# A gated scan and two feed-forward layers on one core: gates and weight sums moved to GpSimd, two plain groups in the second unit in place of three

## The chip, the core and the metric

The kernel runs on one core of a Trainium2 chip. The metric is the device time of one execution in microseconds; before the change it is 1969.47, the median of three runs (1969.35 to 1969.48). The engines are written as in the profile: PE (TensorE's matmuls), PEld (its weight loads), DVE (VectorE), ACT (ScalarE), POOL (GpSimd) and SP, whose queue issues nearly all of the DMAs.

## The reference

```python
def _attn_ref(x, f_logit, lower_bound):          # 2 x 6080 x 256
    sig = 1.0 / (1.0 + np.exp(-f_logit))
    f = lower_bound[None, None, :] + (1.0 - lower_bound[None, None, :]) * sig
    i = 1.0 - f
    for t in range(S):
        h = f[:, t] * h + i[:, t] * x[:, t]
        y[:, t] = h
def _moe_ref(x, w_in, w_out):                    # 12160 x 256, 2048 wide
    h = np.maximum(x @ w_in, 0.0)
    return h * h @ w_out
def _moe2_ref(x, w_in, w_out):
    h = x @ w_in
    g = np.where(h > 0.0, h, alpha * (np.exp(np.minimum(h, 0.0)) - 1.0))
    return g @ w_out
```

The scan feeds the first layer (m = 0), and that one feeds the second (m = 1). All in float32.

## The kernel before, in words

**Tiles.** The 12160 tokens are cut into 12 units: the first has 512 + 384 tokens, all others 512 + 512. Each layer goes unit by unit and, inside a unit, through eight groups g of its 2048 inner columns. The second layer follows the first five units behind.

**Precision.** Each float32 operand of a matmul is split into a high part (rounded to float32r, by ACT or as a DVE cast) and a low part (DVE subtraction, lines 467, 542, 901 and 401). Every product is then three matmuls (`three`, line 854).

**Two forms of a group's first matrix product.** A group multiplies a 2 x 2 block of weights with a 2 x 2 block of inputs (two halves of the tokens, two halves of the 256 inputs). In the *plain* form that is 4 products for each half of the tokens, 8 in all, or 24 matmuls (`add_plain`). In the *other* form it is 7 products, or 21 matmuls (`open_slot`, `add_product`, in the order of `PATTERN`), for which sums and differences of the inputs (lines 601 and 542) and of the weights (`weight_sums`, four 128x128 operations, lines 375 to 378) have to be there first, and the results of which are added up by DVE from PSUM (line 1081). The second matrix product takes 24 matmuls for a group in both forms (line 1138). `plain` (line 243) uses the plain form for the whole of the first unit of the first layer and for the groups below `PLAIN_G` of its second unit.

**Weights.** `add_weights` loads and rebuilds a group's weights. For the first layer it keeps them in DRAM (`keep` in `wd`, `keep_whole` in `rd`); `add_sums` (line 502) later loads `rd`, makes the sums, splits them and writes them to `wd` too. `add_stream` then loads the split weights of each slot from `wd` to `ws`. For the second layer `add_weights` makes the sums itself.

**Scan.** Each unit has four chunks of 256 tokens (`add_scan`, line 693). A chunk is loaded, goes through a tanh on ACT (line 738), two transposes on DVE (line 758, `xT` and `fT`), two gates on 128x256 (line 767, `fT` in place), `feed` (line 775) and two scans (line 788). The first unit has its own path, whose gates are on ACT and DVE.

**Order.** Every step is given to a planner (`Order`) with an engine, an estimated duration and a due time. It runs a simulated clock and writes each engine's instructions in the order in which they came out. On the chip every engine, SP's queue among them, runs its own in that fixed order, and waits at each instruction until its inputs are there. POOL has no step in the plan before the change.

Of the kernel before, what the change touches and what calls it, by code (L numbers as in the profile page):

```python
# [13 lines left out]
ALU = mybir.AluOpType  # L14
PSUM = bass.MemoryType.PSUM

P = 128
# [1 line left out]
CN = 256  # L19
SIZES = ((512, 384), (512, 512))  # L20
LEAD = 2
PLAIN_G = 3
TLATE = 75.0
SLATE = 4.0
GAP = 56
# [41 lines left out]
class Order:  # L67
# [47 lines left out]
    def run(self):  # L115
        steps = self.steps
        after = self.after
        for (tag, k), n in self.first.items():
            steps[n][4].update(self.users.get((tag, k - BUFS[tag]), ()))
            if k and self.first[tag, k - 1] != n:  # L120
                after.add((self.first[tag, k - 1], n))
        for p, n in after:
            steps[n][4].add(p)
        users = [[] for _ in steps]
        wait = [len(s[4]) for s in steps]
        for n, s in enumerate(steps):
            for p in s[4]:
                users[p].append(n)
        free = {"PE": 0.0, "ACT": 0.0, "DVE": 0.0, "SP": 0.0}
        ends = [None] * len(steps)  # L130
        began = [None] * len(steps)
        moved = 0.0
        ready = {e: {} for e in free}

        def offer(n):
            s = steps[n]
            for e in [s[0]] + ([s[5][0]] if s[5] else []):
                t = 0.0
                for p in s[4]:
                    pe, pt = ends[p]  # L140
                    lat = self.LOAD + self.MORE * (pt > 25.0) if pe == "SP" else self.CROSS if pe != e else 0.0 if e == "PE" else self.SAME
                    t = max(t, began[p] if (p, n) in after else pt + lat)
                ready[e][n] = t

        for n, w in enumerate(wait):
            if not w:
                offer(n)
        order = []
        while any(ready.values()):
            best = None  # L150
            for e, r in ready.items():
                if not r:
                    continue
                t0 = max(free[e], min(r.values()))
                n = min((n for n, t in r.items() if t <= t0 + self.HOLD), key=lambda n: steps[n][2])
                if t0 < self.RAMP:
                    late = t0 > self.CALM
                    v = min((n for n, t in r.items() if t <= t0 + self.WAIT[late]), key=lambda n: steps[n][2])
                    if steps[v][2] < steps[n][2] - self.FAR[late]:
                        n = v  # L160
                t0 = max(t0, r[n])
                if best is None or t0 < best[0]:
                    best = (t0, e, n)
            t0, e, n = best
            s = steps[n]
            us = s[1] if e == s[0] else s[5][1]
            free[e] = t0 + us
            began[n] = t0
            ends[n] = (e, t0 + us)
            if s[6]:  # L170
                moved = max(moved, t0 + us / 2) + s[6] / (self.FIRST if moved < 6.0 else self.RATE if moved < 25.0 else self.LATER)
                ends[n] = ("SP", max(moved, t0 + us))
                if e == "SP":
                    free[e] = max(free[e], moved - self.AHEAD)
            for r in ready.values():
                r.pop(n, None)
            order.append((n, e))
            for u in users[n]:
                wait[u] -= 1
                if not wait[u]:  # L180
                    offer(u)
        assert len(order) == len(steps)
        for n, e in order:
            steps[n][3](e)
# [3 lines left out]
def kernel(  # L188
# [11 lines left out]
    nc = tc.nc  # L200
# [3 lines left out]
    KD = D // P  # L204
# [38 lines left out]
    def plain(m, u, g=0):  # L243
        return m == 0 and (u == 0 or u < PLAIN and g < PLAIN_G)

# [4 lines left out]
    rd = [dram.tile([P, 4, P], F32, name=f"rd{g}") for g in range(KG)]  # L250
    xd = [dram.tile([P, KD, sum(ns)], F32, name=f"xd{u}") for u, ns in enumerate(units)]

    def new(tag, shape, dtype=F32):
        return pools[tag].tile(shape, dtype, tag=tag, name=tag)
# [82 lines left out]
    order = Order()  # L337

    def act(n, psum=False):
        return (0.05 if psum else 0.09) + n / 1172  # L340

    def dve(n, fast=False, psum=False):
        return (0.12 if psum else 0.067) + n / (1920 if fast else 960)

    def chain(due, steps):

        left = sum(st[1] + order.SLACK for st in steps)
        for e, us, what, *rest in steps:
            order.add(e, us, due - left, what, *rest)
            left -= us + order.SLACK  # L350
# [3 lines left out]
    def key_of(tag):  # L354
        count[tag] = count.get(tag, -1) + 1
        return tag, count[tag]
# [15 lines left out]
            queue.dma_start(st.rearrange("p k e w -> p k (e w)"), v)  # L372

    def weight_sums(q, a):
        nc.vector.tensor_tensor(q[:, 0], a[:, 0], a[:, 2], op=ALU.add)
        nc.vector.tensor_tensor(q[:, 2], a[:, 1], a[:, 0], op=ALU.subtract)
        nc.vector.tensor_tensor(q[:, 1], q[:, 0], a[:, 1], op=ALU.subtract)
        nc.vector.tensor_tensor(q[:, 3], a[:, 3], q[:, 1], op=ALU.subtract)

    def plain_weights(key):  # L380

# [7 lines left out]
    def add_kept_parts(t, x, key, m, c, at, due):  # L389

        w = key_of("wp")

        def high_part(e):
            t["w" + x] = new("wp", [P, 4, P], F32R)
            if e == "ACT":
                nc.scalar.activation(t["w" + x], t[x], AF.Copy)
            else:
                nc.vector.tensor_copy(t["w" + x], t[x])

        def low_part(e):  # L400
            nc.vector.tensor_tensor(t[x].bitcast(F32R), t[x], t["w" + x].bitcast(F32), op=ALU.subtract)

        def keep(e):
            nc.sync.dma_start(wd[m][c][:, 0, at : at + 4].bitcast(F32), t["w" + x].bitcast(F32))
            nc.sync.dma_start(wd[m][c][:, 1, at : at + 4].bitcast(F32), t[x])

        chain(due, [
            ["DVE", dve(CE, True), high_part, [key], [w], ("ACT", act(CE))],
            ["DVE", dve(CE), low_part, [w], [key]],
            ["SP", 1.0, keep, [w, key], [("wd", m, c, at)], None, 512],  # L410
        ])

    def add_weights(i, m, kind, c, due, wk=None):
# [58 lines left out]
        def keep_whole(e):  # L472
            nc.sync.dma_start(rd[c], t["a"])

        st, a = ("st", i), key_of("a")
        steps = [
            ["SP", 0.475, load, (), [st], None, 512],
            ["ACT", act(CE), scaled, [st], [a]],
            ["ACT", act(CE), low_bits, (), [st]],
            ["DVE", dve(CE), magnitude, [st], [a]],  # L480
            ["DVE", dve(CE), sign, [st], [a]],
        ]
# [2 lines left out]
            del steps[0]  # L485
        if m == 1 and kind == 0:
            q = key_of("a")
            chain(due - 6.0, [*steps, ["DVE", 4 * dve(P), sums, [a], [q]]])
            add_kept_parts(t, "a", a, m, c, 0, due - 2.0)
            add_kept_parts(t, "q", q, m, c, 4, due)  # L490
            return
# [5 lines left out]
        ])  # L497
        if kind == 0:
            order.add("SP", 0.5, due + 16.0, keep, [w], [("wd", m, c, 0)], None, 512)
            order.add("SP", 0.5, due + 10.0, keep_whole, [a], [("rd", c)], None, 256)  # L500

    def add_sums(c, due):

        t = {}

        def load(e):
            t["a"] = new("a", [P, 4, P])
            nc.sync.dma_start(t["a"], rd[c])

        def sums(e):  # L510
            t["q"] = new("a", [P, 4, P])
            weight_sums(t["q"], t["a"])

        a, q = key_of("a"), key_of("a")
        chain(due - 4.0, [
            ["SP", 0.5, load, [("rd", c)], [a], None, 256],
            ["DVE", 4 * dve(P), sums, [a], [q]],
        ])
        add_kept_parts(t, "q", q, 0, c, 4, due)

# [172 lines left out]
    def add_scan(i, u, h, q, due, after=None, from_=None):  # L693
        at, n = chunks(u, h)[q]
# [66 lines left out]
        def gate(c):  # L761
            def go(e):
                f, a, b = t["fT"], ga[:, c : c + 1], gb[:, c : c + 1]
                if e == "ACT":
                    nc.scalar.activation(f[:, c], f[:, c], AF.Identity, scale=a, bias=b)
                else:
                    nc.vector.tensor_scalar(f[:, c], f[:, c], a, b, op0=ALU.mult, op1=ALU.add)  # L767
            return go

        def bound(e):  # L770
# [30 lines left out]
        fs, xs, fT, xT = (("fs", i), ("xs", i), ("fT", i), ("xT", i))  # L801
# [3 lines left out]
        if u == 0:  # L805
# [34 lines left out]
            ["ACT", act(N), tanh, (), [fs]],  # L840
            ["DVE", dve(N), turn("xs", "xT"), [xs], [xT], None, 0, after],
            ["DVE", dve(N), turn("fs", "fT"), [fs], [fT], None, 0, after],
            *(["DVE", dve(n), gate(c), [("bound",)], [fT]] for c in range(KD)),
            ["DVE", dve(N), feed, [fT], [xT]],
            *(["DVE", 0.1 + n / 490, scan(c), [fT, xT, ("carry",), ("scan",), *opened], [F, (*F, c), ("scan",)]] for c in range(KD)),
            *([["DVE", 0.1, carry_on, [F], [("carry",)]]] if h * q else []),
# [418 lines left out]
    def begin_unit(s):  # L1265
# [12 lines left out]
        elif u in mixed and m == 0:  # L1278
            if s == (m, u, None, PLAIN_G):
                add_later_parts(u, mixed[u], s)  # L1280
# [49 lines left out]
```

## Time and profile before

| | |
|---|---|
| median of three runs | 1969.47 us (1969.35 to 1969.48) |
| span of the profiled execution (first to last instruction) | 1968.4 us |
| median less span: what lies around the span | 1.07 us |
| busy: PE, ACT, DVE, POOL | 1955.5, 1627.1, 1498.6, 0.7 us |
| PE waits for other engines and DMAs, whole run | 8.4 us in 5 waits |

The page gives the profiled execution by its span alone; its own time is taken as that span and the 1.07 us around it, which is the median of the runs. PE's busy time counts a matmul from its modelled start to its modelled end, and matmuls overlap in the pipeline, so the number of matmuls times the step between them says more of PE than the busy share.

### The profile page before, as it was taken

Reading aid. Unit: us, or ns where it says so; the run is one execution under the profiler, and the core shown is the slowest. Engines: PE = TensorE matmul, PEld = TensorE weight load, DVE = VectorE, ACT = ScalarE, POOL = GpSimd, SP = SyncE. Lnnn points to the kernel's source line nnn. Section 1 sums busy time; section 2 is a strip of 40 time slices with the busy share of each in tenths; the row PEclk is TensorE's granted clock in tenths of the full one; section 3 lists DMA queues with packets and bytes.
Section 4 is the critical chain, followed back from the end, with each engine's and each line's share of the span. In section 5 each row is a group of like instructions: output and inputs, shape, how many; then the busy total and the mean of one; then the engine's idle time right before and its main releaser. Section 6 shows DMA issues by size and latency. Waiting matters only on the chain.

```text
span 1968.4 us, 23749 instructions
## 1 busy us (share of the span) xinstructions
PE 1955.5 (99%) x8713; PEld 1631.7 (83%) x8713; DVE 1498.6 (76%) x1933; ACT 1627.1 (83%) x2181; POOL 0.7 (0%) x6
## 2 busy tenths in 40 slices
PE   8999999999999999999999999999999999999999
PEld 7888888888888888888888888888888888888888
DVE  7998899867876876777777687687775668778686
ACT  8989999888888878878878887887887878878786
POOL 0000000000000000000000000000000000000000
PEclk9999999999999999999999999999999999999999
DMA  8876675532533434353254343334423324243332
GB/s 259 241 225 210 206 226 176 170 128 94 145 128 115 114 119 137 102 149 132 81 146 128 113 131 113 126 104 126 137 94 102 126 99 137 94 134 99 113 116 74
DMA packets 228868, 269.21 MB, mean 137 GB/s; under 512 B 151952, under 2 KB 154512, under 8 KB 228752
## 3 DMA queue, kind: packets, MB, share of 16 engines
q1 hardware_dynamic: 226752, 267.24, 43.2%
q8 instruction: 68, 1.11, 0.2%
q10 hardware_dynamic: 2000, 0.46, 0.1%
q14 instruction: 48, 0.39, 0.1%
HBM read 223.87 MB, written 43.78 MB: 136 GB/s over the span
## 4 chain that ended last, share of the span: by engine, by line
PE 99%; DVE 1%; DMA 0%; ACT 0%; issue 0%; SPq 0%; DVEq 0%
PE a L1138 53%; PE c L856 46%; DMA st<-in_moe_w_in_dram 0%; DVE F L788 0%; DVE a L432 0%; DVE a L435 0%; DVE xT L749 0%; DVE o L1177 0%; DVE xa L542 0%; SPq L701 0%; DVE F L467 0%; DVE fT L767 0%; DVE ws L467 0%; ACT a L426 0%; ACT st L429 0%
## 5 line engine op out<-in xcount | busy, mean ns | idle before, releaser
L1138 PE MATMUL a<-g,wo 128*128 128x512 f32 (+2 forms) x4608 | 1155.7, 387 | 0.0
L1138 PEld LDWEIGHTS a<-g,wo 128*128 128x128 f32 x4608 | 863.8, 188 | 171.2
L1074 ACT ACTIVATE r<-c 128x512 f32<-128x512 f32 (+1 forms) x724 | 423.4, 585 | 251.0 <-PE c L856 245.0
L901 DVE TENSOR_TENSOR g<-r,g 128x1024 fp32r<-128x1024 f32 (+2 forms) x382 | 461.6, 1208 | 142.1 <-ACT g L896 134.4
L1081 DVE TENSOR_TENSOR r<-c,r 128x512 f32<-128x512 f32 (+1 forms) x543 | 371.6, 684 | 191.7 <-PE c L856 187.7
L896 ACT ACTIVATE g<-r 128x1024 fp32r<-128x1024 f32 (+2 forms) x382 | 402.9, 1055 | 67.1 <-PE a L1138 50.4
L856 PE MATMUL c<-xa,ws 128*128 128x512 f32 (+2 forms) x1713 | 445.3, 387 | 1.1 <-DVE ws L467 0.6
L856 PEld LDWEIGHTS c<-xa,ws 128*128 128x128 f32 x1713 | 320.5, 188 | 65.9 <-DVE ws L467 1.0
L856 PE MATMUL c<-xb,ws 128*128 128x512 f32 (+2 forms) x1146 | 316.3, 386 | 0.0
L891 DVE SCALAR_TENSOR_TENSOR r<-e,r 128x1024 f32<-128x1024 f32 (+1 forms) x190 | 230.8, 1215 | 105.3 <-ACT e L888 105.3
L856 PE MATMUL c<-xc,ws 128*128 128x512 f32 (+1 forms) x1098 | 307.1, 388 | 0.0
L856 PEld LDWEIGHTS c<-xb,ws 128*128 128x128 f32 x1146 | 214.6, 188 | 42.0
L856 PEld LDWEIGHTS c<-xc,ws 128*128 128x128 f32 x1098 | 206.1, 188 | 41.9
L881 ACT ACTIVATE r<-r 128x1024 f32<-128x1024 f32 (+1 forms) x192 | 201.0, 1048 | 0.3
L888 ACT ACTIVATE e<-e 128x1024 f32<-128x1024 f32 (+1 forms) x190 | 198.5, 1045 | 0.7
L885 ACT ACTIVATE e<-r 128x1024 f32<-128x1024 f32 (+1 forms) x190 | 197.2, 1042 | 0.4
L875 ACT ACTIVATE r<-r 128x1024 f32<-128x1024 f32 x85 | 89.4, 1051 | 0.0
L601 DVE TENSOR_TENSOR F<-F 128x512 f32<-128x512 f32 (+1 forms) x92 | 62.9, 683 | 1.0
L788 DVE TENSOR_TENSOR_SCAN F<-fT,F,xT 128x256 f32<-128x256 f32 (+1 forms) x72 | 52.2, 736 | 0.7
L878 ACT ACTIVATE r<-r 128x512 f32<-128x512 f32 x85 | 52.7, 620 | 0.0
L542 DVE TENSOR_TENSOR xa<-F,xa 128x512 fp32r<-128x512 f32 (+3 forms) x49 | 44.9, 923 | 0.4
L767 DVE TENSOR_SCALAR fT<-fT,ga,gb 128x256 f32<-128x256 f32 x90 | 33.7, 404 | 0.9
(72 smaller groups left out, 608.1 us busy)
## 6 DMA issues: line engine op xcount, KB each, us to landing
ws<-wd SPq DMA_DIRECT2D x181, 896.0 KB, 4.9
xd<-o SPq DMA_DIRECT2D x46, 256.0 KB, 2.8
fs<-in_f_logit_dram SPq DMA_DIRECT2D x176, 64.0 KB, 2.3
xs<-in_x_dram SPq DMA_DIRECT2D x176, 64.0 KB, 2.6
F<-xd SPq DMA_DIRECT2D x22, 512.0 KB, 4.7
out_dram<-o SPq DMA_DIRECT2D x88, 128.0 KB, 5.3
st<-in_moe_w_in_dram SPq DMA_DIRECT2D x16, 512.0 KB, 5.5
st<-in_moe_w_out_dram SPq DMA_DIRECT2D x16, 512.0 KB, 4.8
```

What stands on the lines that cost most here:

```text
L601: nc.vector.tensor_tensor(f[:, to], f[:, i], f[:, k], op=ALU.subtract)
L856: nc.tensor.matmul(out, lhsT=ws[:, p, w], rhs=xs[:, r, v], start=start and q == 0, stop=stop and q == 2, skip_group_check=check,)
L875: nc.scalar.activation(r_t[0], r_t[0], AF.Relu)
L881: nc.scalar.activation(r_t[0], r_t[0], AF.Square)
L885: nc.scalar.activation(t["e"], r_t[0], AF.Relu, scale=-1.0)
L888: nc.scalar.activation(t["e"], t["e"], AF.Exp, scale=-1.0)
L891: nc.vector.scalar_tensor_tensor(r_t[0], t["e"], 1.0, r_t[0], op0=ALU.subtract, op1=ALU.max)
L896: nc.scalar.activation(g_t[s, which][:, 0], r_t[0], AF.Copy)
L901: nc.vector.tensor_tensor(g_t[s, which][:, 1], r_t[0], g_t[s, which][:, 0].bitcast(F32), op=ALU.subtract)
L1074: nc.scalar.activation(r[0][:, i], t[A], f)
L1081: nc.vector.tensor_tensor(r[:, i], t[tag], r[:, i], op=ALU.add)
L1138: nc.tensor.matmul(a, lhsT=y, rhs=v, start=begin and jj == 0 and p == 0, stop=end and jj == len(mine) - 1 and p == 2, skip_group_check=True,)
```

## The change

It does four things. The gates of all units but the first, and the sums of the weights of both layers, are GpSimd instructions (`engine.tensor_scalar` and `nc.gpsimd.tensor_tensor`), and the planner gets a POOL engine with an estimate of its own. `PLAIN_G` is 2, so that group 2 of the second unit has the form with seven products. The write of the whole weights to `rd` is due 7 us earlier.

```diff
-PLAIN_G = 3
+PLAIN_G = 2
...
-        free = {"PE": 0.0, "ACT": 0.0, "DVE": 0.0, "SP": 0.0}
+        free = {"PE": 0.0, "ACT": 0.0, "DVE": 0.0, "POOL": 0.0, "SP": 0.0}
...
+    def pool(n):
+        return 0.15 + n / 900
...
     def weight_sums(q, a):
-        nc.vector.tensor_tensor(q[:, 0], a[:, 0], a[:, 2], op=ALU.add)
-        nc.vector.tensor_tensor(q[:, 2], a[:, 1], a[:, 0], op=ALU.subtract)
-        nc.vector.tensor_tensor(q[:, 1], q[:, 0], a[:, 1], op=ALU.subtract)
-        nc.vector.tensor_tensor(q[:, 3], a[:, 3], q[:, 1], op=ALU.subtract)
+        nc.gpsimd.tensor_tensor(q[:, 0], a[:, 0], a[:, 2], op=ALU.add)
+        nc.gpsimd.tensor_tensor(q[:, 2], a[:, 1], a[:, 0], op=ALU.subtract)
+        nc.gpsimd.tensor_tensor(q[:, 1], q[:, 0], a[:, 1], op=ALU.subtract)
+        nc.gpsimd.tensor_tensor(q[:, 3], a[:, 3], q[:, 1], op=ALU.subtract)
...
-            chain(due - 6.0, [*steps, ["DVE", 4 * dve(P), sums, [a], [q]]])
+            chain(due - 6.0, [*steps, ["POOL", 4 * pool(2 * P), sums, [a], [q]]])
...
-            order.add("SP", 0.5, due + 10.0, keep_whole, [a], [("rd", c)], None, 256)
+            order.add("SP", 0.5, due + 3.0, keep_whole, [a], [("rd", c)], None, 256)
...
-            ["DVE", 4 * dve(P), sums, [a], [q]],
+            ["POOL", 4 * pool(2 * P), sums, [a], [q]],
...
-                    nc.vector.tensor_scalar(f[:, c], f[:, c], a, b, op0=ALU.mult, op1=ALU.add)
+                    engine = nc.gpsimd if e == "POOL" else nc.vector
+                    engine.tensor_scalar(f[:, c], f[:, c], a, b, op0=ALU.mult, op1=ALU.add)
...
-            *(["DVE", dve(n), gate(c), [("bound",)], [fT]] for c in range(KD)),
+            *(["POOL", pool(n), gate(c), [("bound",)], [fT]] for c in range(KD)),
```

In the changed kernel's rows line numbers are 3 higher from line 345 and 4 higher from line 768 on: 542 is 545, 758 is 761, 775 is 779, 788 is 792, 901 is 905, 1081 is 1085, 1138 is 1142. In all, 88 gates and 64 sums stand on POOL, and DVE has 88 and 64 fewer; matmuls are 8710, from 8713.

**A chunk of the scan in a late unit, DVE.** Before:

```order
L758 STREAM_TRANSPOSE xT<-xs 128x8x2x32
L758 STREAM_TRANSPOSE fT<-fs 128x8x2x32
L767 TENSOR_SCALAR fT<-fT,ga,gb 128x256 x2
L775 SCALAR_TENSOR_TENSOR xT<-fT,xT 128x512
L788 SCALAR_TENSOR_TENSOR F_8677<-fT,F_8677,xT 128x256
L901 TENSOR_TENSOR g<-r,g 128x1024
L1081 TENSOR_TENSOR r<-c_8903,r 128x512
```

The same place of the changed kernel:

```order
L761 STREAM_TRANSPOSE xT<-xs 128x8x2x32
L761 STREAM_TRANSPOSE fT<-fs 128x8x2x32
L779 SCALAR_TENSOR_TENSOR xT<-fT,xT 128x512
L792 SCALAR_TENSOR_TENSOR F_8680<-fT,F_8680,xT 128x256
L905 TENSOR_TENSOR g<-r,g 128x1024
L1085 TENSOR_TENSOR r<-c_8904,r 128x512
```

The two gates are gone from DVE's queue, and in this chunk nothing has come in their place: `feed` stands right behind the transpose, and waits for POOL.

**Where the second unit takes up the other form, DVE.** `F_829` holds the scan's result of the second unit, `xa`, `xb` and `xc` its split inputs; the rows of 128x512 for `xb` and `xc` are the raw second half, the row of 128x1024 is the differences of products 4 and 3. The changed kernel:

```order
L545 TENSOR_TENSOR xb<-F_829,xb 128x512
L545 TENSOR_TENSOR xc<-F_829,xc 128x512
L470 TENSOR_TENSOR wo_71<-a,wo_71 128x2x256
L604 TENSOR_TENSOR F_829<-F_829 128x512
L905 TENSOR_TENSOR g<-r,g 128x2x384
...
L404 TENSOR_TENSOR a<-a,wp 128x512 x2
L905 TENSOR_TENSOR g<-r,g 128x1024
L761 STREAM_TRANSPOSE fT<-fs 128x8x2x32
L545 TENSOR_TENSOR xb<-F_829,xb 128x1024
```

Between the second row and the last stand 14 instructions; before the change 33 stood there, 12 of them sums and 2 gates.

**The same place on POOL**, from its first gates on:

```order
L771 TENSOR_SCALAR fT<-fT,ga,gb 128x256 x3
L378 TENSOR_TENSOR a<-a 128x128
L379 TENSOR_TENSOR a<-a 128x128
L380 TENSOR_TENSOR a<-a 128x128
L381 TENSOR_TENSOR a<-a 128x128
L771 TENSOR_SCALAR fT<-fT,ga,gb 128x256 x3
L378 TENSOR_TENSOR a<-a 128x128
```

Gates and sums share one queue: a gate of the second unit's second chunk stands behind the first group's four sums, which wait for their own load.

## Rows read from the trace of the kernel before

**Rows 1.** The page: span, busy time of engines, granted clock by slice.

```profile
span 1968.4 us, 23749 instructions
...
PE 1955.5 (99%) x8713; PEld 1631.7 (83%) x8713; DVE 1498.6 (76%) x1933; ACT 1627.1 (83%) x2181; POOL 0.7 (0%) x6
...
PEclk9999999999999999999999999999999999999999
```

**Rows 2.** Waits of PE: line, waited for, us in total, times, longest.

```profile
PE c L712 <- DMA fs<-in_f_logit_dram: 6.6, 2, 3.9
PE a L712 <- DMA fs<-in_f_logit_dram: 0.7, 1, 0.7
PE c L856 <- DVE ws L467: 0.6, 1, 0.6
PE c L856 <- DVE xa L542: 0.5, 1, 0.5
```

**Rows 3.** The chain that ended last: start us, us, what.

```profile
21.60 6.78 PE c L856 x34
...
118.62 2.04 PE a L1138 x9
...
128.82 2.04 PE a L1138 x9
...
1954.07 9.13 PE a L1138 x45
```

**Rows 4.** Windows, four of 20 us from 60 to 140 us: busy us of each engine.

```profile
sum 80.00, PE 80.00 PEld 68.91 DVE 77.96 ACT 68.36 POOL 0.00; mean PE 20.00 PEld 17.23 DVE 19.49 ACT 17.09 POOL 0.00
```

**Rows 5.** Groups of DVE instructions, 60 to 140 us: count, busy us, mean ns.

```profile
L767 DVE TENSOR_SCALAR fT<-fT,ga,gb 128x256 f32<-128x256 f32 x16 | 6.2, 400 | 0.0
...
L378 DVE TENSOR_TENSOR a<-a 128x128 f32<-128x128 f32 x8 | 2.3, 292 | 0.3
...
L375 DVE TENSOR_TENSOR a<-a 128x128 f32<-128x128 f32 x8 | 2.3, 281 | 0.9 <-DMA a<-rd 0.9
```

**Rows 6.** Groups of the whole run: gates on ACT, what POOL ran.

```profile
L765 ACT ACTIVATE fT<-fT,gb,ga 128x256 f32<-128x256 f32 (+1 forms) x6 | 3.4, 565 | 0.2
...
masks.py:199 POOL TENSOR_SCALAR_AFFINE_SELECT one<-one 128x128 f32<-128x128 f32 x1 | 0.3, 294 | 0.1
masks.py:197 POOL MEMSET one<- 128x128 f32 x1 | 0.2, 205 | 0.3 <-POOLq L1316 0.3
...
L1316 POOL MEMSET const-uint8-127<- 128x1 uint8 x1 | 0.1, 102 | 0.0
```

**Rows 7.** Timeline of a late chunk: start us, us, engine, line, what.

```profile
1026.03 0.67 DVE L758 STREAM_TRANSPOSE fT<-fs 128x512 f32<-128x512 f32 x1
...
1027.50 0.69 DVE L775 SCALAR_TENSOR_TENSOR xT<-fT,xT 128x512 f32<-128x512 f32 x1
...
1029.60 1.23 DVE L901 TENSOR_TENSOR g<-r,g 128x1024 fp32r<-128x1024 f32 x1 [0.61 <-ACT g L896]
1030.74 0.68 DVE L1081 TENSOR_TENSOR r<-c,r 128x512 f32<-128x512 f32 x1
...
1032.38 0.84 PE L856 MATMUL c<-xc,ws 128*128 128x512 f32 x3
```

**Rows 8.** Timeline where the second unit changes form.

```profile
94.45 2.88 PE L856 MATMUL c<-xa,ws 128*128 128x512 f32 x12
...
96.16 0.69 DVE L542 TENSOR_TENSOR xc<-F,xc 128x512 fp32r<-128x512 f32 x1
...
99.27 0.86 PE L856 MATMUL c<-xb,ws 128*128 128x512 f32 x3
...
114.45 1.22 DVE L542 TENSOR_TENSOR xb<-F,xb 128x1024 fp32r<-128x1024 f32 x1
...
117.78 0.84 PE L856 MATMUL c<-xb,ws 128*128 128x512 f32 x3
```

**Rows 9.** Timeline of SP's queue: the first DMA at which its order changes.

```profile
19.29 0.39 SPq L366 DMA_DIRECT2D st<-in_moe_w_out_dram  x1
```

## The prediction

> **What bounds the kernel now.** Read the page first. PE is busy for 1955.5 of 1968.4 us, its granted clock is at the upper level, 2.4 GHz, in every slice, DVE has 24% to spare over the run, and POOL ran 0.7 us [rows 1]. So the question is only what PE still waits for, and the view of waits answers it: 8.4 us in five waits, two for the first tokens' loads and two for the first unit's weights and inputs [rows 2]. The chain of waits agrees: from 21.60 us to PE's last work (1954.07 + 9.13 = 1963.2) it is PE alone, one stretch of matmuls after the other [rows 3]. The time is therefore a count of matmuls times a step. The chain gives the step: a group of the form with seven products, with its second product, is 21 + 24 = 45 matmuls and comes back after 128.82 - 118.62 = 10.20 us [rows 3], so one matmul of 512 columns takes 10.20 / 45 = 0.2267 us. (The 0.39 us that the groups of instructions give for one matmul is a length in a pipeline, not a step.)
>
> Nothing that is taken off DVE shortens that chain by itself. What it can do is keep PE fed where DVE was nearly full: from 60 to 140 us DVE was busy for 77.96 of 80 us [rows 4], while PE never waited. There the change works.
>
> **The change part by part.**
>
> *Two plain groups, not three.* Group 2 of the second unit takes 21 matmuls in place of 24 for its first product, and 24 for its second as before. PE loses 3 matmuls: 3 x 0.2267 = 0.68 us, straight off the chain. DVE gets three more additions from PSUM (0.68 us each, as in [rows 7]), ACT four evacuations more of one kind and four fewer of another; both have room.
>
> *Gates and sums off DVE.* In 60 to 140 us DVE ran 16 gates (6.2 us) and 8 sets of four sums (four groups of 2.3 us, 9.2 us) [rows 5]; 15.4 us at most go from 78, since busy times of neighbours overlap a little. On the path of PE this is worth nothing: it waited for none of it. Over the run DVE loses 88 gates of 0.40 us and 64 sums of 0.29 us, some 54 us.
>
> *The same on POOL.* The trace has no gate on POOL, so I bound one. Below: a MEMSET of 128 columns took 0.205 us and one of a single column 0.102, which is 0.81 ns a column, so 256 columns take 0.31 us; it only writes. Nearest, since it reads and writes: the AFFINE_SELECT of 128 columns, 0.294 us, is 1.51 ns a column, so a gate takes 0.49 us. Above: twice that rate, 0.88 us. ACT's gate takes 0.565 us, inside these bounds [rows 6]. A sum has 128 columns and two inputs: 0.205 below, 0.49 with the read counted twice, 0.88 above. I take 0.49 us for both, as the nearest row has it. 152 of them are 74 us of 1968 on an engine that did nothing.
>
> *The wait that this adds.* `feed` now waits on DVE for two gates on POOL, and everything behind it on DVE waits too. In the late chunk, DVE's transpose ends at 1026.70 and `feed` starts at 1027.50: the gates cost 0.80 us [rows 7]. On POOL they cost 2 x 0.49 and two handovers; the trace has none with POOL, but DVE took 0.04 us after ACT in this very stretch (an estimate of 0.2 us would be generous). That is 1.06 us, with 0.2 us each 1.38: `feed` comes 0.26 to 0.58 us later. Behind it stand the scan and line 901, before which DVE sat idle for 0.61 us [rows 7], which covers it. If a gate took 0.88 us, `feed` would come 1.04 us later with the short handover, 901 0.43 us later, and then the addition of line 1081; it ended at 1031.42, and the matmul that takes that bank again (product 1) starts at 1032.38, 0.96 us after [rows 7]. So PE still would not wait. Cost 0; the cover is the 0.61 and the 0.96 us, and it is gone when a gate costs more than (0.80 + 0.61 + 0.96 - 0.08) / 2 = 1.14 us.
>
> *The second unit changes form one group earlier.* One plain group is gone ahead of it, so two things are wanted earlier. The raw second half (`xb`, `xc`) was wanted at 99.27 us and is wanted where group 2's plain product started, at 94.45, 4.82 us earlier. `xc` was ready at 96.85, and PE took it 0.70 us after `xb`, at 99.97; now it is wanted at 95.15 [rows 8]. That needs 1.70 us off DVE's work; 8 of the 16 gates and 3 of the 8 sets stood ahead, 8 x 0.40 + 12 x 0.287 = 6.6 us [rows 5]. Margin 4.9 us. The differences (128x1024) were wanted at 117.78 and are wanted 48 x 0.2267 = 10.9 us earlier, at 106.9 [rows 8]. The changed order has 14 instructions between `xc` and them; 11 of about 0.69 us, three of 1.23 us and their own 1.22 us are 12.5 us [rows 7, 8], counted from 96.85 - 6.6 = 90.25 that is 102.8. Margin 4.1 us. Cost 0, between 0 and some 3 us if the freed time is partly lost.
>
> *The earlier write to `rd`.* On SP it moves ahead of a load of weights, first at 19.29 us [rows 9]. An issue takes about 0.4 us, so the load comes that much later; from 21.60 us on PE waited for no weight [rows 3]. Three such places lie in the first unit: 0 to 1.2 us, I take 0.
>
> **Sum.** 1968.4 + 1.07 us around the span is the median of the runs, 1969.47. Less 0.68 it is **1968.8 us**, 0.03% less. About 0.2%, 3.9 us, is what a measurement of this kernel can tell from no change, so my forecast is "no change that can be told". Its own range, with that cost at 1.2 us and the runs' spread of 0.1 to both sides, is 1968.7 to 1970.1.
>
> **The rivals.**
>
> *A. The handover comes late.* POOL's queue is in order, and a gate of the second chunk stands behind the first four sums, which wait for their load. If this, or the load, costs more than the margin of 4.1 us, PE pays the rest one for one. For: DVE did idle 0.9 us for that very load [rows 5]. Against: twice that and four sums (2.0 us) are still inside. I price it in the middle of what stays under 3.9 us, +1.9: 1970.7.
>
> *B. POOL and DVE block each other.* DVE frees time, but each POOL instruction makes DVE stand still for as long. Up to `xc` that is 8 gates and 12 sums, 20 x 0.49 = 9.8 us back for 6.6 us saved; `xc` then comes at 96.85 - 6.6 + 9.8 = 100.05 and is wanted at 95.15: PE waits 4.9 us, 1973.7, slower. At ACT's price for a gate (0.565) it is 6.4 us, 1975.2. It decides from half of it on: with 0.245 us of standstill for each instruction the 4.9 us of margin are just used up. Later the kernel has idle DVE time at each chunk, and loses nothing. For: DVE is near its limit there [rows 4]. Against: while `feed` waits for a gate, DVE stands idle and cannot be blocked. The trace has no two of them side by side.
>
> The Trainium skill has such a rule ("SBUF — State Buffer", section "Who interferes with whom"): a DVE instruction with two inputs in SBUF contends with a GpSimd instruction that reads SBUF, and the second to issue waits. By that rule DVE's subtractions and `feed` would meet gates and sums, its transposes and its additions from PSUM would not, and the time would be B's instead of mine. No run here shows it.
>
> *C. A gate on POOL is slow.* Above 1.14 us a gate, each of the 36 chunks of the units behind the third costs PE what is over. At 1.4 us that is 2 x 0.26 x 36 = 18.7 us: 1987.5, slower. For: no row prices it. Against: it would be nearly five times the AFFINE_SELECT for twice the columns.
>
> *D. Faster by over 0.2%.* That would need 3.9 us off PE. PE's waits are 8.4 us, all in the first unit [rows 2], which the change leaves as it is. Only matmuls count, and three go. It would be 1965.5 or less.
>
> **How the numbers follow.** Forecast 0.62; A 0.18; B 0.10; C 0.07; D 0.03. Faster 0.03, same 0.62 + 0.18 = 0.80, slower 0.10 + 0.07 = 0.17. The likeliest time is 1968.8. The range goes from 1968.3, a little under the forecast, through A up to B's 1973.7, say 1974; outside it are C, half of B and D, 0.15.
>
> **What would show it.** Right: PE 8710 matmuls, its waits the same four kinds and about 8.4 us, the form of 45 matmuls in the second unit from about 104 us on, 74 us or less on POOL, some 1445 us on DVE. In the chunk, DVE idle before `feed`, waiting for POOL, and no wait of PE for `r` behind it. A shows as one wait of PE near 84, 94 or 107 us for `xa`, `xb`, `xc` or `ws`. B shows as gates, sums or subtractions much longer between 60 and 110 us than alone, C as gates over 1.1 us and PE waiting for line 1081's result in every unit. The prediction is wrong if PE's waits grow by over 4 us, or if the step of a matmul changes.

## The result and the profile after

| | before | after |
|---|---|---|
| median | 1969.48 us (1969.35 to 1970.0) | 1980.14 us (1979.02 to 1980.69, 5 runs) |
| ratio | | 1.0051, 95% interval 1.0041 to 1.0062 |
| span of the profiled execution | 1968.4 us | 1977.4 us (of 1979.35) |

The change makes the kernel 0.5% slower, 10.7 us. The prediction was 1968.8, with 1968.3 to 1974.0 as its range: wrong, and by far more than the 3.9 us that can be told from no change.

First the page of the changed kernel, which answers to [rows 1]: span, busy time, and two of its costliest groups (busy us, mean ns, idle before and what ended it).

```profile
span 1977.4 us, 23864 instructions
...
PE 1959.2 (99%) x8710; PEld 1631.9 (83%) x8710; DVE 1462.4 (74%) x1782; ACT 1625.3 (82%) x2185; POOL 103.1 (5%) x158
...
L771 POOL TENSOR_SCALAR fT<-fT,ga,gb 128x256 f32<-128x256 f32 x88 | 62.5, 719 | 1128.1 <-DVE fT L761 1128.1
...
L779 DVE SCALAR_TENSOR_TENSOR xT<-fT,xT 128x512 f32<-128x512 f32 x44 | 30.6, 694 | 36.1 <-POOL fT L771 35.9
```

The three matmuls are gone, DVE is relieved of 36 us, and `feed` waits for POOL 36 us in all. That is not where the time went. PE's waits after the first unit tell it (line, waited for, us, times, longest); before, none but the first unit's [rows 2]:

```profile
PE a L1142 <- ACT wo L464: 3.8, 1, 3.8
PE c L860 <- DVE r L1085: 0.7, 2, 0.4
PE a L1142 <- DVE g L905: 0.6, 1, 0.6
```

PE is held up from 87 us on. Windows of 20 us from 60 to 140 us show the place (busy us of each engine, then granted clock):

```profile
80.00:100.00 20.00, 15.59 (x63) 12.05 (x62) 15.99 (x25) 13.49 (x22) 9.20 (x13) 0.91 0.70 230
100.00:120.00 20.00, 20.00 (x95) 17.18 (x94) 13.50 (x17) 15.31 (x24) 8.53 (x15) 1.00 0.68 211
...
sum 80.00, PE 74.78 PEld 62.28 DVE 59.25 ACT 62.45 POOL 32.35; mean PE 18.70 PEld 15.57 DVE 14.81 ACT 15.61 POOL 8.09
```

DVE, busy for 77.96 of these 80 us before [rows 4], is now busy for 59.25: 18.7 us less, more than the 15.4 that went to POOL. It is not short of time, it stands and waits. The timeline of the changed kernel shows for what (start us, us, engine, line; in brackets the idle time before and what ended it):

```profile
72.20 5.52 SPq L737 DMA_DIRECT2D xs<-in_x_dram  x8
...
78.45 1.02 SPq L511 DMA_DIRECT2D a<-rd  x2
...
83.19 0.46 POOL L378 TENSOR_TENSOR a<-a 128x128 f32<-128x128 f32 x1 [5.30 <-issue]
...
84.57 0.46 POOL L381 TENSOR_TENSOR a<-a 128x128 f32<-128x128 f32 x1
85.06 0.63 ACT L399 ACTIVATE wp<-a 128x512 fp32r<-128x512 f32 x1 [4.96 <-POOL a L381]
...
85.60 0.83 ACT L900 ACTIVATE g<-r 128x768 fp32r<-128x768 f32 x1
...
86.46 1.05 DVE L905 TENSOR_TENSOR g<-r,g 128x768 fp32r<-128x768 f32 x1 [3.90 <-ACT g L900]
...
87.57 2.17 PE L1142 MATMUL a<-g,wo 128*128 128x384 f32 x11 [0.64 <-DVE g L905]
87.81 2.84 POOL L771 TENSOR_SCALAR fT<-fT,ga,gb 128x256 f32<-128x256 f32 x2
...
95.59 0.63 ACT L464 ACTIVATE wo<-a 128x512 fp32r<-128x512 f32 x1 [0.68 <-DVE a L438]
...
96.27 4.70 PE L1142 MATMUL a<-g,wo 128*128 128x512 f32 x12 [3.77 <-ACT wo L464]
...
97.73 0.55 POOL L378 TENSOR_TENSOR a<-a 128x128 f32<-128x128 f32 x1 [7.07 <-DMA a<-rd]
98.24 1.17 POOL L379 TENSOR_TENSOR a<-a 128x128 f32<-128x128 f32 x1
```

Read it downwards. The loads of the whole weights (`a<-rd`) leave SP behind eight loads of `xs`, at 78.45. POOL's sums start at 83.19. ACT has the split of these sums (`wp`) ahead of a `g` in its fixed order and stands 4.96 us; DVE needs that `g` and stands 3.90; PE needs DVE's part of it. From 86.46 on DVE works off its order without another wait, scans and the parts of the next chunk first; the rebuilding of the next `wo` has its place behind them, and PE waits 3.77 us for it. The gates behind the two sets of sums, at 87.81, end at 90.65 and hold up nothing here: `feed` comes at 91.11, right behind DVE's own transpose.

That wait costs more than its length. Small windows (same columns; the number after POOL's is the granted clock):

```profile
94.00:96.00 2.00, 0.00 (x0) 0.00 (x0) 2.00 (x5) 1.31 (x3) 0.00 (x0) 1.00 0.71 138
96.00:98.00 2.00, 1.73 (x3) 1.00 (x4) 2.00 (x5) 1.93 (x5) 0.27 (x1) 0.54 0.44 124
98.00:100.00 2.00, 2.00 (x7) 1.61 (x6) 2.00 (x3) 1.57 (x2) 2.00 (x3) 0.61 0.00 0
100.00:102.00 2.00, 2.00 (x11) 1.61 (x10) 1.97 (x3) 1.59 (x3) 1.07 (x2) 1.00 0.10 39
```

After PE's idle time the clock is near its lower level, 1.2 GHz, for some three microseconds. The twelve matmuls from 96.27 took 4.70 us; twelve of 512 columns took 2.88 before [rows 8]. The difference is 1.8 us, a part of which is a second wait, for the low part of `wo`. The waits above are 5.1 us together, so 6.9 us of the 9.0 by which the profiled span grew are accounted for. Some 0.9 us more is lost after 140 us: from there to 400 us PE ran 1145 matmuls, against 1149 before. The rest was not traced to a place.

### The profile page after: what moved, and what is told of

It reads as the page before. It is cut to its first block, busy times and chain, and to the rows that moved or that the text cites. A ratio compares the mean times of both kernels' runs of the same rounds, so it can differ in the third digit from the quotient of the medians.

```text
span 1977.4 us, 23864 instructions
## 1 busy us (share of the span) xinstructions
PE 1959.2 (99%) x8710; PEld 1631.9 (83%) x8710; DVE 1462.4 (74%) x1782; ACT 1625.3 (82%) x2185; POOL 103.1 (5%) x158
## 4 chain that ended last, share of the span: by engine, by line
PE 95%; DVE 2%; DMA 1%; issue 1%; POOL 1%; ACT 0%; SPq 0%; DVEq 0%; POOLq 0%; ACTq 0%
PE a L1142 51%; PE c L860 45%; DMA ws<-wd 0%; DVE F L792 0%; DMA st<-in_moe_w_in_dram 0%; DMA wd<-wp 0%; DMA xs<-in_x_dram 0%; DVE g L905 0%; DVE F L604 0%; POOL a L381 0%; DVE a L435 0%; DVE a L438 0%; SPq L737 0%; POOL a L380 0%; DVE xa L545 0%
## 5 line engine op out<-in xcount | busy, mean ns | idle before, releaser
L771 POOL TENSOR_SCALAR fT<-fT,ga,gb 128x256 f32<-128x256 f32 x88 | 62.5, 719 | 1128.1 <-DVE fT L761 1128.1
L779 DVE SCALAR_TENSOR_TENSOR xT<-fT,xT 128x512 f32<-128x512 f32 x44 | 30.6, 694 | 36.1 <-POOL fT L771 35.9
```

## The experiments

All times are medians; a ratio is to the kernel before on the same chip, 95% interval in brackets. "Two" and "three" are the plain groups of the second unit; "apart" is the constant `SLATE`, explained below.

| run | plain | gates | sums | other edit | us | ratio |
|---|---|---|---|---|---|---|
| before | three | DVE | DVE | | 1969.5 | |
| after | two | POOL | POOL | `rd` earlier | 1980.1 | 1.0051 |
| 1 | two | DVE | DVE | `rd` earlier | 1978.6 | 1.0043 [1.0031, 1.0056] |
| 2 | two | DVE | POOL | `rd` earlier | 1979.7 | 1.0052 [1.0039, 1.0064] |
| 3 | two | POOL | DVE | `rd` earlier | 1975.1 | 1.0029 [1.0018, 1.0039] |
| 4 | three | POOL | POOL | `rd` earlier | 1971.8 | 1.0010 [1.0001, 1.0019] |
| 5 | two | DVE | DVE | | 1981.2 | 1.0056 [1.0044, 1.0069] |
| 6 | two | POOL | POOL | `rd` earlier, `a<-rd` loads earlier | 1979.2 | 1.0048 [1.0035, 1.0060] |
| 7 | two | POOL | POOL | `rd` earlier, POOL priced higher | 1975.1 | 1.0028 [1.0018, 1.0039] |
| 8 | three | DVE | DVE | `rd` earlier | 1969.5 | 1.0000 [0.9991, 1.0009] |
| 9 | two | DVE | DVE | one set of sums left out | 1983.1 | 1.0068 [1.0055, 1.0081] |
| 10 | two | DVE | DVE | 1 apart | 1974.1 | 1.0023 [1.0013, 1.0032] |
| 11 | three | POOL | POOL | `rd` earlier, POOL priced higher | 1972.5 | 1.0013 [1.0004, 1.0022] |
| 12 | two | POOL | DVE | `rd` earlier, POOL priced higher | 1974.7 | 1.0025 [1.0016, 1.0035] |
| 13 | two | POOL | DVE | `rd` earlier, 1 apart | 1972.2 | 1.0014 [1.0005, 1.0023] |
| 14 | two | POOL | POOL | `rd` earlier, 1 apart | 1977.9 | 1.0041 [1.0029, 1.0054] |
| 15 | two | DVE | DVE | 1 apart, two sets later | 1978.1 | 1.0044 [1.0031, 1.0056] |
| 16 | three | DVE | DVE | 1 apart | 1975.4 | 1.0029 [1.0019, 1.0040] |
| 17 | two | DVE | DVE | 2 apart | 1970.9 | 1.0006 [0.9998, 1.0015] |
| 18 | two | POOL | POOL | `rd` earlier, 2 apart | 1978.8 | 1.0047 [1.0033, 1.0060] |

### GpSimd or the form? (runs 1 to 4)

Runs 1 to 3 put gates and sums, gates alone, or sums alone of the changed kernel back on VectorE; run 4 sets three plain groups again.

```diff
-        nc.gpsimd.tensor_tensor(q[:, 0], a[:, 0], a[:, 2], op=ALU.add)
+        nc.vector.tensor_tensor(q[:, 0], a[:, 0], a[:, 2], op=ALU.add)
...
-            *(["POOL", pool(n), gate(c), [("bound",)], [fT]] for c in range(KD)),
+            *(["DVE", dve(n), gate(c), [("bound",)], [fT]] for c in range(KD)),
...
-PLAIN_G = 2
+PLAIN_G = 3
```

> Gates and sums back on DVE; two plain groups and the earlier write to rd stay. Theory 1 (POOL's instructions cost what was lost: they are slow beside DVE, and what waits for them comes late): PE has no stall behind the start, 0.7 us faster than before, 1968.8 us. Theory 2 (the earlier change of form alone is too tight, on whatever engine): PE waits between 84 and 100 us as in the changed kernel, 1975 to 1980 us.

> Only the gates go back to DVE; the sums stay on POOL. Theory 1a (the sums are the cause: ACT's high part of the sums stood waiting for POOL for 5.0 us at 80 to 85 us, with everything that PE needed behind it): still 1975 to 1980 us, with that wait of ACT. Theory 1b (the gates are the cause: 1.4 us each beside DVE, and the scans behind them): below 1971 us, and no PE wait over 0.5 us after 40 us.

> Only the sums go back to DVE; the gates stay on POOL. Theory 1a (sums): below 1971 us. Theory 1b (gates): 1975 to 1980 us. If both kernels with one half on POOL are near 1969, the loss needs both, in one queue: gates that stand behind sums that wait for their load.

> Gates and sums on POOL, but three plain groups as before. Theory 1: the loss stays, 1976 to 1981 us. Theory 3 (POOL's lateness costs only because the other form comes 10.9 us earlier): at most 1972 us, PE's wait for wo near 92 us gone.

Run 1: 1978.6 without a single instruction of the change on POOL. Most of the loss needs no GpSimd. Run 4: with three groups GpSimd costs 2.3 us. Runs 2 and 3: the sums on POOL cost 1.1 us (run 2 against 1, inside the intervals), the gates on POOL gain 3.5 (run 3 against 1). The two do not add up: beside gates on POOL the sums there cost 5.0 us (the changed kernel against run 3), and beside sums on POOL the gates there gain nothing (against run 2).

### The form alone (runs 5 and 8)

The kernel before with one of the change's other two edits at a time:

```diff
-PLAIN_G = 3
+PLAIN_G = 2
```

```diff
-            order.add("SP", 0.5, due + 10.0, keep_whole, [a], [("rd", c)], None, 256)
+            order.add("SP", 0.5, due + 3.0, keep_whole, [a], [("rd", c)], None, 256)
```

> The kernel before with two plain groups in the second unit in place of three, and nothing else: the gates and sums stay on VectorE, the weights' half sums (rd) are written as late as before. Theory 2 (the change of form one group earlier is too tight on whatever engine): 1975 to 1980, as the run without GpSimd (1978.6), with waits of TensorE at 84 to 100 us. A rival, that the rd write which was brought forward does part of it (it takes SyncE's queue ahead of the loads of xs): under 1974, the waits at 84 to 100 us under 2 us in sum. The prediction's cost of 0: 1968.9.

> The kernel before with the earlier write of the half sums alone (due + 3 in place of due + 10), three plain groups and everything on VectorE. The prediction's term: 0, at most 1.2: 1969.5 to 1970.7. If the earlier write takes SyncE's queue from loads that TensorE waits for: 1971 to 1973, with waits for ws, xa or r in the second unit.

Run 8 gives the earlier write its price in the kernel before: nothing. Run 5 gives the whole loss and a little more, 11.7 us, from one digit. With the earlier write beside it (run 1) it is 2.6 us less, but the intervals overlap; whether the write has another price in this order is not shown. PE's waits in run 5:

```profile
PE a L1138 <- ACT wo L461: 6.0, 1, 6.0
PE c L856 <- DVE r L1081: 2.1, 2, 1.5
```

DVE's waits, 60 to 140 us; before, the same wait is 0.9 us [rows 5]:

```profile
DVE a L375 <- DMA a<-rd: 7.9, 6, 2.2
```

And its timeline at the wait for `wo`:

```profile
78.20 1.71 SPq L508 DMA_DIRECT2D a<-rd  x2
...
83.48 0.29 DVE L375 TENSOR_TENSOR a<-a 128x128 f32<-128x128 f32 x1 [1.57 <-DMA a<-rd]
...
84.42 0.69 DVE L432 SCALAR_TENSOR_TENSOR a<-a,st 128x512 int32<-128x512 int32 x1
...
85.35 0.69 DVE L435 SCALAR_TENSOR_TENSOR a<-st,a 128x512 int32<-128x512 int32 x1
...
86.07 0.63 ACT L461 ACTIVATE wo<-a 128x512 fp32r<-128x512 f32 x1 [0.17 <-DVE a L435]
...
86.75 3.62 PE L1138 MATMUL a<-g,wo 128*128 128x512 f32 x8 [6.04 <-ACT wo L461]
```

The rebuilding of `wo` (lines 432 and 435) stands on DVE behind sums whose load was issued 5.3 us before, and DVE stands 1.57 us for it. DVE's other waits since 60 us are 0.54 and 1.54; what is left of PE's 6.04 us lies in the place that `wo` has in DVE's order. The chain is like that of the changed kernel, with DVE's sums in POOL's place.

### Three repairs (runs 6, 7, 11, 12)

Run 6 gives the loads of `a<-rd` a due time of their own. Runs 7, 11 and 12 raise the planner's price of POOL to what the trace shows beside DVE; run 11 has three plain groups, and run 12 the sums on VectorE.

```diff
+        order.add("SP", 0.5, due - 30.0, load, [("rd", c)], [a], None, 256)
         chain(due - 4.0, [
-            ["SP", 0.5, load, [("rd", c)], [a], None, 256],
             ["POOL", 4 * pool(2 * P), sums, [a], [q]],
```

```diff
-        return 0.15 + n / 900
+        return 0.2 + n / 256
...
-            ["POOL", 4 * pool(2 * P), sums, [a], [q]],
+            ["POOL", 3.3, sums, [a], [q]],
```

> The changed kernel with the loads of the weights' half sums (a<-rd) given a place of their own on SyncE, some 26 units of the planner's time earlier, so that they stand ahead of the loads of xs that wait for buffers. If the chain xs loads, then a<-rd, then GpSimd's sums, then ScalarE's copy wp<-a, then g is what TensorE waits for, the waits at 84 to 100 us fall from 5 us to under 2 us and the clock stays at its upper level: 1972 to 1975. If the sums were only one of several works that VectorE, ScalarE and GpSimd have too much of in this stretch, the waits come back for another operand (r, scans, wo): 1977 to 1981.

> The changed kernel with the planner's prices of GpSimd's operations raised to what the trace shows beside VectorE: a gate of 256 columns 1.2 in place of 0.43, four sums 3.3 in place of 1.7. If the planner's wrong price puts work in a bad order (ScalarE's copy wp<-a ahead of g, gates behind sums), waits fall: 1972 to 1976. If the stretch has too much work or too late loads in any order: 1977 to 1981.

> The changed kernel with three plain groups (1971.8) and the planner's prices of GpSimd's operations as the trace shows them beside VectorE (gate 1.2, four sums 3.3). If the 2.3 us that GpSimd costs there come from steps placed by a price that is too low: 1969.3 to 1970.5. If they come from VectorE and GpSimd slowing each other: 1971 to 1973.

> The changed kernel (two plain groups) with the sums on VectorE, gates on GpSimd (1975.1) and a gate priced at 1.2. If price and place are what is left: 1970 to 1973. If the early form is too tight by itself: 1974 to 1978.

Run 6 misses: the first of the two loads left at 72.32 us and its sums began at 76.01, in place of 78.45 and 83.19, and PE waited 3.4 us for `wo` and 1.3 for its low part all the same; the load is not the one link to mend. The price helps run 7 by 5 us but not run 11 (0.7 us more than run 4) nor run 12 (0.4 less than run 3, inside the intervals). A wrong price is not the cause by itself; each price gives another order, better or worse.

### Too much work, or the due times? (runs 9, 10, 15 to 17)

The planner's due time for a set of sums comes from two lines (before, 1221 and 1223):

```python
weights.append((T0 + (T3 - T0) * (g + 0.8) / KG, "sums", 0, g, None))
...
weights.append((in_due[0, 1, None, g] - 10.0 - SLATE * (KG - 1 - g), "sums", 0, g, None))
```

The first is for groups that are plain in the second unit, the second for the others. With three plain groups, group 2's sums fall under the first line and are spread over the way to the third unit. With two they fall under the second, with `SLATE` 4 due 10 + 4 x 5 = 30 units ahead of their slot, in the stretch where DVE is full. Run 9 leaves that set's arithmetic out, loads its weights and writes them back as they are, and the planner makes a new order; runs 10 and 17 set `SLATE` to 1 and 2; run 15 also puts the third unit's first two sets later (0.8 becomes 3.8); run 16 sets `SLATE` to 1 in the kernel before.

```diff
-SLATE = 4.0
+SLATE = 1.0
```

```diff
+        if c == PLAIN_G:
...
+            chain(due, [
+                ["SP", 0.5, load, [("rd", c)], [a], None, 256],
+                ["SP", 1.0, keep, [a], [("wd", 0, c, 4)], None, 512],
+            ])
+            return
```

> The kernel before with two plain groups, with the arithmetic of one set of sums left out: that of the group that changes its form (group 2 of the second unit), some 2 us of VectorE and 0.6 us of ScalarE; its half sums are loaded and written back in place of the sums, so that group's weights are not those of the reference. If the stretch from 60 to 100 us has simply one set of sums too much work: the waits there fall from 8 us to under 2 us, 1970 to 1973. If what counts is the order in which the planner sets the loads, wo and g: 1976 to 1982, waits of other operands.

> The kernel before with two plain groups, with the sums of later groups due later (1 unit of the planner's time for each group that is still to come, in place of 4). If the sums due early (those of group 3 and of the third unit beside those of group 2) crowd out the wo weights at 80 to 87 us: 1970 to 1975. If the work of group 2 alone is too much before its stream load: 1977 to 1983, with waits for ws or wo.

> Everything on VectorE, two plain groups, sums due later as at 1974.1, and the sums of the third unit's first two groups put later by three eighths of the way to that unit. If VectorE's load from 80 to 131 us is what is left: 1970 to 1973. If the waits are set by the order of r beside the scans: 1973.5 to 1976.

> The kernel before, three plain groups, with the sums due later (1 in place of 4). If the due times are tuned to the form, so that any other set of them leaves stalls with either form: 1971 to 1976. If before has room whatever the due times and only the early form is tight: 1969.2 to 1970.2.

> The kernel before with two plain groups and sums due 2 units apart, between 4 (1981.2) and 1 (1974.1). If the cost follows how early the sums are due: 1975 to 1979. If each set of due times gives an order of its own with stalls that don't follow the size of the step: outside of that.

Run 9 speaks against too much work as the cause: with some 2 us less of it on DVE the time is 1983.1, and PE still waits 3.7 us for `wo`. Run 17 is the decisive one. With two plain groups, everything on VectorE and 2 units apart, the time is 1970.9, against 1981.2 with 4 apart, and its interval takes in the time before. Its waits of PE after the first unit, and its windows' sum from 60 to 140 us:

```profile
PE c L856 <- ACT r L1074: 0.8, 1, 0.8
```

```profile
sum 80.00, PE 78.96 PEld 67.16 DVE 77.77 ACT 68.82 POOL 0.00; mean PE 19.74 PEld 16.79 DVE 19.44 ACT 17.20 POOL 0.00
```

The same sum of run 5:

```profile
sum 80.00, PE 71.83 PEld 60.85 DVE 71.34 ACT 60.19 POOL 0.00; mean PE 17.96 PEld 15.21 DVE 17.84 ACT 15.05 POOL 0.00
```

In the bad order DVE is busy for 6.4 us less than in the good one, and waits 7.9 us for `a<-rd`, against 0.5 us in run 17. Runs 5 and 17 have the same instructions and differ in one due-time constant: it is order, not load. That it is the due time of the one set that changed its rule is argued; no run moves that set alone back.

Run 16 says that this is not a fault of the earlier form alone: with three plain groups, 1 apart costs 5.9 us, and DVE waits 6.5 us for `a<-rd` there. The cost does not follow the size of the step (4, 2, 1 apart: 11.7, 1.3, 4.5 us over before), against the first of run 17's two cases. Each due time makes an order of its own; of those tried, 4 was good with three plain groups and 2 with two. Nor does every bad order show by the wait for `a<-rd`: in run 10 that is 0.7 us, DVE is busy for 77.90 of the 80 us, and PE waits 3.7 us for `r`. Run 15 misses as well: 80 to 100 us come free of waits, and PE waits 5.6 us for `r` from 117 us on.

### GpSimd, with the other due times (runs 13, 14, 18)

Runs 13 and 14 are run 3 and the changed kernel with 1 apart, run 18 the changed kernel with 2 apart.

> Two plain groups, the sums due later as in the run at 1974.1, and the gates on GpSimd (sums on VectorE). If the 3.7 us of waits left there are VectorE's load: 1969 to 1972, waits for r under 1.5 us. If GpSimd's gates lengthen VectorE's own operations as much as they relieve it: 1973 to 1976.

> The changed kernel with the sums due later (1 in place of 4) and nothing else. If the order alone made its loss at 84 to 100 us: no wait over 1 us for wo or g there and 1970 to 1974. If GpSimd's slow sums beside VectorE keep them late: 1975 to 1980.

> The changed kernel, gates and sums on GpSimd, with the sums due 2 units apart in place of 4. If the due times are the cause and GpSimd costs what it does with three plain groups (2.3 us): 1971 to 1974. If GpSimd's gates and sums keep their operands late in any order: 1975 to 1980.

Run 18 misses what run 17 promised: the due times that mend the form on VectorE leave 1978.8, 8.0 us over run 17, with GpSimd and the earlier write. Run 14 against 13: the sums on POOL cost 5.7 us. Run 13 against 10: the gates on POOL gain 2.0, but the earlier write came with them. Run 14 fits neither of its cases: PE waits for `wo` and `g` by 0.2 us each, as in the first, and the time is the second's. All its waits behind the first unit are 2.7 us; after three of them close together, from 107 to 111 us, the granted clock is 0.50 from 112 to 114 us. DVE's waits in run 18, 60 to 140 us:

```profile
DVE g L905 <- ACT g L900: 6.8, 3, 4.1
DVE a L404 <- ACT wp L399: 6.3, 3, 2.9
DVE wp L401 <- POOL a L381: 5.8, 2, 3.4
```

and ACT's:

```profile
ACT wp L399 <- POOL a L381: 10.2, 4, 3.5
```

The last is 10.4 us in the changed kernel; runs 13 and 17 have no wait of DVE for `g` in these 80 us. It is the chain of the first timeline: POOL's sums late, ACT standing at their split, `g` behind it. PE's longest wait behind the first unit is 2.0 us there, for `xb`.

So there are two faults, and either is enough for a loss. With the old due times the form alone costs 11.7 us (run 5; 9.1 with the `rd` edit, run 1) and POOL adds little (10.7 in the changed kernel); with due times that suit the form, POOL and the `rd` edit together cost 8.0. No run has that edit alone at 2 apart; where it was tried, it cost nothing (run 8) or came with 2.6 us less (run 1 against 5, inside the intervals). No version here beats the kernel before, and there is little to win: before, PE waited for nothing after the first unit, and three matmuls are 0.7 us.

What stays open: what of POOL's 8 us is its own slowness and what the order that the planner makes with POOL in it. Every run that moved work to another engine also got another order. Not tried: the gates alone on POOL at 2 apart. The 1.3 us between run 17 and before are not cleared up either; PE waits 0.8 us there for `r`, and the interval takes in zero.

## Why the prediction was wrong, point by point

**Three matmuls, 0.68 us:** the count is right, 8710; the time is too small to see.

**The step that failed is "The second unit changes form one group earlier ... Cost 0, between 0 and some 3 us".** It measured 11.7 us (run 5), or 9.1 with the earlier write (run 1). The step counted what the form's own operands need (`xb`, `xc` and the differences) and took the margins from the order of before. In these runs and in the changed kernel PE waited for none of these; it waited for `g`, `wo` and `r`, operands that the change does not touch. The diff's one digit also moves a set of sums to another due-time rule, and with it loads on SP, splits on ACT and everything behind them. A margin read from the old order holds only while the order holds. The step also paid DVE's freed time in as if DVE could use it; DVE was waiting instead (59.25 us busy, where the removal alone would leave some 62.6). So the margins were not there either. In the changed kernel:

```profile
96.07 0.68 DVE L545 TENSOR_TENSOR xc<-F,xc 128x512 fp32r<-128x512 f32 x1
```

`xc` was ready at 96.75 us, as late as before (96.85), where the step had 90.25 and PE was to take it at 95.15. PE took it at 101.50 only, since `wo` had held PE up before.

**The price of POOL, 0.49 us: a little low alone, much too low in the full stretch.** After 400 us, and from 60 to 140 us, the groups of the changed kernel (count, busy us, mean ns, idle before):

```profile
L771 POOL TENSOR_SCALAR fT<-fT,ga,gb 128x256 f32<-128x256 f32 x48 | 27.9, 591 | 951.4 <-DVE fT L761 951.4
...
L771 POOL TENSOR_SCALAR fT<-fT,ga,gb 128x256 f32<-128x256 f32 x12 | 14.5, 1214 | 69.1 <-DVE fT L761 69.1
```

A gate takes 0.59 us late in the run and 1.21 us in the full stretch, above the upper bound of 0.88. A sum is 0.46 us where DVE stands and up to 1.17 beside it (98.24 in the timeline). POOL was busy for 103 us, not 74 or less, and DVE lost 36 us, not some 54.

**The wait that this adds, cost 0: right for the late chunks.** In one of the changed kernel:

```profile
1034.33 0.67 DVE L761 STREAM_TRANSPOSE fT<-fs 128x512 f32<-128x512 f32 x1
...
1035.17 1.09 POOL L771 TENSOR_SCALAR fT<-fT,ga,gb 128x256 f32<-128x256 f32 x2 [19.03 <-DVE fT L761]
...
1036.30 0.69 DVE L779 SCALAR_TENSOR_TENSOR xT<-fT,xT 128x512 f32<-128x512 f32 x1 [1.30 <-POOL fT L771]
```

`feed` starts 1.30 us after the transpose, in place of 0.80 [rows 7]: 0.50 us later, inside the predicted 0.26 to 0.58, and the view of waits has no wait of PE after 140 us. The four matmuls that PE is behind from 140 to 400 us lie in earlier chunks; with gates alone (run 3) or sums alone (run 2) on POOL it is one.

**The earlier write to `rd`, 0: right in the order of before** (run 8); beside two plain groups the time was 2.6 us lower with it (run 1 against 5), inside the intervals.

**Rival A had the place and not the price.** It named waits of PE near 84 and 94 us behind sums that wait for their load, and they came at 87.57 and 96.27, though for `g` and `wo`. Its +1.9 was set in the middle of what would still be no change. That is no measurement: nothing in the rows bounded the lateness, so the range should have reached further.

**Rival B: the blocking is there, on the other side.** It had each POOL instruction hold DVE for 0.49 us, and `xc` come late. The scan on DVE in the full stretch, 60 to 140 us, first of the changed kernel, then of the one before:

```profile
L792 DVE TENSOR_TENSOR_SCAN F<-fT,F,xT 128x256 f32<-128x256 f32 x6 | 4.8, 813 | 0.0
```

```profile
L788 DVE TENSOR_TENSOR_SCAN F<-fT,F,xT 128x256 f32<-128x256 f32 x10 | 7.4, 744 | 0.0
```

That is 0.07 us more; POOL's gate takes 0.62 more than late in the run. POOL pays most. The Trainium skill ("SBUF — State Buffer", section "Who interferes with whom") has a VectorE instruction with two SBUF inputs and a GpSimd instruction that reads SBUF lock each other out, so that the second waits. The trace agrees that the two lengthen each other, by the numbers above, but not that DVE loses what B gave it: nearly all of it falls on GpSimd here.

**Rival C fell**: gates are over 1.14 us on the mean of the full stretch, not in every unit; after 400 us they take 0.59.

**The time around the span** was put at 1.07 us, the median less the profiled span. In all runs whose time and span are both known, an execution takes 1.73 to 1.95 us more than its span, whatever the kernel, the one before among them; the profiled execution of before was so probably 0.7 us above its median. The forecast is the median less 0.68 and does not hang on it. A slip that changes nothing: the prediction gives the first tokens' loads two of PE's five waits, and [rows 2] has three.

## What to carry to other kernels

Where a planner writes the order of every queue, an edit is priced by the order that comes out: compare the new order of each engine, from the loads to the matmul, and look for instructions that now stand behind a load just issued. Here a stretch where DVE was nearly full and PE never waited had no reserve for another order; a due time that was set for the old form has to be set again with the new one, before the form or the engine is blamed. A second engine does not relieve the first by taking its work alone: what it makes must not come late to its place in the fixed order of a third, as the sums did on ACT. Moving the gates gained 3.5 us against the same kernel without (run 3 against 1); moving the sums gained in no run.

## What the runs showed of the hardware

- A GpSimd gate of 256 columns takes 0.55 us where DVE stands still (two in 1.09 us) and 1.4 us beside DVE's work (two in 2.84 us at 87.81); DVE's own scan is lengthened by 0.07 us on the mean from 60 to 140 us.
- After 3.8 us without a matmul the granted clock fell to 0.54 for the next window of 2 us and was 1.00 again after about four; in run 12 it fell to 0.50 from 94 to 96 us after waits of 1.6 and 0.4 us close together, while run 3 kept 1.00 after 1.2 and 0.5 us. In run 14 it fell to 0.50 from 112 to 114 us after waits of 0.4, 0.9 and 0.7 us between 107 and 111 us.
